# LSH attention with an MLP on one core: the hashes of batches 2 and 3 made in one stretch each, from block transposes in place, with the squares behind them

## The chip, the cores and the metric

One Trainium2 chip, one of its cores. The metric is the device time of one execution in microseconds (us), the median of several runs. The kernel before: 305.03 us (three runs, 304.65 to 305.60).

## The reference

```python
q_bits = (einsum('bhsd,dk->bhsk', q, proj) > 0)     # 6 bits for each token and head
k_bits = (einsum('bhsd,dk->bhsk', k, proj) > 0)
mask = q_bucket[:, :, :, None] == k_bucket[:, :, None, :]
scores = where(mask, q @ k.T / sqrt(D), -1e9)
attn = exp(scores - max) / (sum + 1e-9)
x = (attn @ v).transpose(0, 2, 1, 3).reshape(B, S, H * D)
xn = (x - mean) / sqrt(var + 1e-6) * g_ln
out = x + relu(xn @ w_ch1) @ w_ch2
```

B = 4 batches, H = 8 heads, S = 768 tokens, D = 64, so x is (4, 768, 512); the hidden width is 2048. A query sees only the keys whose 6 hash bits equal its own. All inputs and the output are f32.

## The kernel before, in words

**Chunks and steps.** The work goes in 12 chunks, numbered 0 to 11: 4 batches of 3 chunks of 256 tokens. A chunk has 12 attention units, three for each of four pairs of heads. A unit is a scores step S (4 matmuls, L513, into a tile of the PSUM pool ps_sc, two buffers), an exponential on ACT (L519) and a values step A (8 matmuls, L534, into ps_av). After a pair's third A, DVE divides (L564 to L572) and the pair's part of x is done. The MLP of a chunk runs one chunk later: `norm` on DVE (L626 to L628) and a transposing DMA on SP's queue (L637, xnT), 8 up steps U (8 matmuls each, L653, evicted by DVE L132 and ACT L136 in turn as hbuf), and in the chunk after that 8 down steps D (4 matmuls each, L675; four make one tile o, which DVE adds to x at L680). Up and down tiles, the hash and the share take their PSUM from one pool, ps_mm, with two buffers.

**What prepares a batch.** Each batch comes in two halves of four heads. For batches 2 and 3 each preparing step is a letter with two digits, batch and half: L loads q and k (four DMAs of 384 KB on SP, L147), W loads v (L182); N casts q and k to bf16 on POOL (L270), T transposes them by a DMA into the operand tile `slots` (L294), O places the odd tokens (L194). The hash: B is four block transposes of 32x32 on DVE (L275), from the natural tiles `qnat`, `knat` to tiles `bt`; H is the matmuls of the transposed tile with the projection (L313; 16 in the program and 32 records in the trace for a half), a threshold pass and a scaling on DVE (L321, L324) and a write of the bits to DRAM (L326, bits_d); J reads them back into `slots` (four DMAs, L333). V casts the values on POOL (L419) and sums them; E is the share, one matmul (L433) whose result DVE copies to vsum (L434). Q is four squares in place over q and k, on ACT (L218), whose sums go to the tile `sq`; a reduce of sq (L721), two small DMAs on POOL (L723, L725) and a second reduce (L733) give the flag that chooses at the very end between this kernel and a general path.

**The order.** Chunks 0 to 2 follow an order written by hand. From the third on, `interleave` goes through the units: S of the next unit, then A of this one, with fillers between them, spread by their costs. The fillers of a chunk are `norm`, the four or so last D steps of the chunk before, U steps, and the preparing steps that `plan` names for that chunk: three texts, early | late | end, which are mixed evenly with the first four tail steps, the other four, and the ups. `alone` gives steps that stand right after a unit's S: twelve places, one for each unit. Each engine takes its instructions in the order of its own list. Steps of batches 2 and 3 are kept in the order of the program; a scheduler orders the rest by priority.

Of the kernel before, what the change touches and what calls it, by code (L numbers as in the profile page):

```python
# [9 lines left out]
F32 = mybir.dt.float32  # L10
BF16 = mybir.dt.bfloat16
# [17 lines left out]
def kernel(  # L29
# [11 lines left out]
    nc = tc.nc  # L41
    P = 128

    B, H, S, D = q.shape
# [3 lines left out]
    NC = S // P  # L48
# [5 lines left out]
    CT = TT * P  # L54
# [26 lines left out]
    NG, DG = P // 32, D // 32  # L81
    proj4 = consts.tile([P, DG, 32], F32)
# [23 lines left out]
    for i in range(2):  # L106
# [3 lines left out]
    work = main.enter_context(tc.tile_pool(name="work", bufs=2))  # L110
    bounce = main.enter_context(
        tc.tile_pool(name="bounce", bufs=2, space=bass.MemoryType.DRAM)
    )
    ps_mm = main.enter_context(
        tc.tile_pool(name="ps_mm", bufs=2, space=bass.MemoryType.PSUM)
    )
    attn = ExitStack()
    nat = attn.enter_context(tc.tile_pool(name="nat", bufs=4))
    ps_sc = attn.enter_context(
        tc.tile_pool(name="ps_sc", bufs=2, space=bass.MemoryType.PSUM)  # L120
    )
# [76 lines left out]
    class Prep:  # L198
# [72 lines left out]

        def blocks(self, half, a, j):

            bt = work.tile([P, 2, NC, DG, 32], F32, tag="qkT", bufs=4, name="bt")
            done = nc.vector.transpose(  # L275
                out=bt.rearrange("p h c e j -> p (h c e j)"),
                in_=self.tiles[half]["qk"[a]][:, 2 * j : 2 * j + 2].rearrange(
                    "p h c d -> p (h c d)"
                ),
            )  # L280
            if self.b > 1:
                tc.keep_in_program_order(done)
            self.bt[half, a, j] = bt

        def pair_places(self, half):

# [16 lines left out]
            dst = self.pair_places(half)  # L303
            copy_by(eng, dst[0:D, :, 1, :], dst[D:P, :, 0, :])

        def hashes(self, half):

            NT_ = NC * 32
            hp = ps_mm.tile([P, 2, NT_], F32, tag="mm", name="hash")
            for a in range(2):  # L310
                for e in range(DG):
                    for g in range(4):
                        nc.tensor.matmul(  # L313
                            hp[32 * g : 32 * (g + 1), a, :],
                            proj4[:, e, :],
                            self.bt[half, a, g // 2][:, g % 2, :, e, :],
                            start=(e == 0), stop=(e == DG - 1),
                            skip_group_check=True,
                        )
            bits = work.tile([P, 2, NT_], BF16, tag="bits", name="bits4")  # L320
            nc.vector.tensor_scalar(  # L321
                bits, hp, scalar1=0.0, scalar2=0.5, op0=AOP.is_gt, op1=AOP.subtract
            )
            nc.vector.tensor_scalar_mul(bits, bits, 2.0 * BIT)  # L324
            bd = bounce.tile([P, 2 * NT_], BF16, tag="bits", name="bits_d")
            nc.sync.dma_start(out=bd, in_=bits.rearrange("p a n -> p (a n)"))  # L326
            self.bd[half] = bd

        def bits_home(self, half):

# [39 lines left out]
        def head_rows(self, h, engs):  # L370

            W = HS // 2
            for y, eng in zip((2, 3, 0, 1), engs):
                a, part = y // 2, y % 2
                dst = self.sl[D:K1, h, a].rearrange("p (par u t) -> p par u t", par=2, u=2)
                copy_by(eng, dst[:, :, part, :], self.head_bits[h][32 * y : 32 * y + n_bits])
# [87 lines left out]
        def part(self, kind, half):  # L464

            if kind == "T":
                return [(0, lambda: self.operands(half))]
            if kind in "Oo":
                return [(0, lambda: self.odd_tokens(half, "S" if kind == "O" else "G"))]
            if kind == "H":  # L470
                return [(1300, lambda: self.hashes(half))]
            if kind == "J":
                return [(0, lambda: self.bits_home(half))]
            if kind == "N":
                return [(0, lambda a=a: self.narrow(half, a)) for a in range(2)]
            if kind in "BK":
                return [
                    (0, lambda a=a, j=j: self.blocks(half, a, j))
                    for a in range(kind == "K", 2) for j in range(2)
                ]  # L480
            if kind == "E":
                return [(110, lambda: self.share(half))]
            if kind == "L":
                return [(0, lambda: self.load(half))]
            if kind == "W":
                return [(0, lambda: self.load_v(half))]
            if kind == "V":
                return [(0, lambda: self.values(half)), (0, lambda: self.value_sums(half))]
            return [
                (0, lambda a=a, j=j: self.squares(half, a, j)) for a in range(2) for j in range(2)  # L490
            ]
# [88 lines left out]
    def mlp_steps(b, t, x):  # L580
# [84 lines left out]
        def down(i, part):  # L665
            cut = 2 if (b, t, i) == (B - 1, NT - 1, TT - 1) else 1
            per = 4 // cut
            width = d_model // cut
            cols = slice(part // per * width, (part // per + 1) * width)
            if part % per == 0:  # L670
                st["o"] = ps_mm.tile([P, width], F32, tag="mm", name="o2")
            o2 = st["o"]
            step = NH // per
            for nt in range(part % per * step, (part % per + 1) * step):
                nc.tensor.matmul(  # L675
                    o2, st["h"][:, nt, i * P : (i + 1) * P], w2_sb[:, nt, cols],
                    start=(nt == 0), stop=(nt == NH - 1),
                )
            if part % per == per - 1:
                nc.vector.scalar_tensor_tensor(  # L680
                    x[:, i, cols], o2, st["rs"][:, i : i + 1], x[:, i, cols],
                    op0=AOP.mult, op1=AOP.add,
                )
                nc.sync.dma_start(
                    out=out[b].rearrange("(p c) d -> p c d", p=P)[:, CMAP[b][t * TT + i], cols],
                    in_=x[:, i, cols],
                )

        ups = [(900, lambda n2=n2: up(n2)) for n2 in range(NH // 2)]
        downs = [  # L690
            (870, lambda i=i, part=part: down(i, part)) for i in range(TT) for part in range(4)
        ]
        return (0, norm), ups, downs, (first_stats, first_norm, first_trans)
# [127 lines left out]
    def first_two():  # L821
# [106 lines left out]
    plan = {  # L928
# [7 lines left out]
    }  # L936

    def prepare(text):
# [6 lines left out]
    alone = {  # L945
        2: "Q01 QQQQ..",
        3: "B20 Q10 Q.Q.Q.Q.BBBB",
        4: "B21 Q11 Q.Q.Q.Q.BBBB",
        5: "Q20 Q..Q..Q..Q..",
        6: "B30 Q21 BBBBQ.Q.Q.Q.",  # L950
        7: "B31 Q30 BBBBQ.Q.Q.Q.",
        8: "Q31 Q..Q..Q..Q..",
    }

    def spread(text):
# [237 lines left out]
```

## Time and profile before

| | us |
|---|---|
| median of three runs | 305.03 |
| profiled execution | 305.38 |
| its span | 303.7 |
| busy PE | 295.2 |
| busy ACT | 215.6 |
| busy DVE | 179.8 |
| busy POOL | 91.3 |

The span runs from the first to the last instruction of the profiled execution; 1.7 us of that execution's time lie around it. Rows of the trace give the start in the span, the duration, the engine (PE matmuls, PEld weight loads, DVE, ACT, POOL; SPq and POOLq are DMA issues), the line, the operation, and the tiles written and read. A bracket at the end gives the engine's idle time before the row and what ended it. A matmul group's duration overlaps the next group's start, since matmuls are pipelined, so steps on PE are taken from start to start.

The chunks that the change touches start, by their second scores step, at 95.69 (chunk 4), 119.31 (5), 143.37 (6), 167.20 (7), 191.03 (8), 213.11 (9), 235.18 (10).

### The profile page before, as it was taken

Reading aid. Unit: us, or ns where it says so; the run is one execution under the profiler, and the core shown is the slowest. Engines: PE = TensorE matmul, PEld = TensorE weight load, DVE = VectorE, ACT = ScalarE, POOL = GpSimd, SP = SyncE. Lnnn points to the kernel's source line nnn. Section 1 sums busy time; section 2 is a strip of 40 time slices with the busy share of each in tenths; the row PEclk is TensorE's granted clock in tenths of the full one; section 3 lists DMA queues with packets and bytes.
Section 4 is the critical chain, followed back from the end, with each engine's and each line's share of the span. In section 5 each row is a group of like instructions: output and inputs, shape, how many; then the busy total and the mean of one; then the engine's idle time right before and its main releaser. Section 6 shows DMA issues by size and latency. Waiting matters only on the chain.

```text
span 303.7 us, 7929 instructions
## 1 busy us (share of the span) xinstructions
PE 295.2 (97%) x3285; PEld 224.7 (74%) x3309; DVE 179.8 (59%) x409; ACT 215.6 (71%) x273; POOL 91.3 (30%) x117
## 2 busy tenths in 40 slices
PE   8999899999999999999999999999999999999995
PEld 5677788578688688678678678679679678687564
DVE  1998678845659459634964954633733734646322
ACT  4899986967788778669578687879677667665020
POOL 3559490685403424500831730200300200201100
PEclk9999999999999999999999999999999999999999
DMA  6999999588296379777487274330110210200302
GB/s 197 367 311 252 260 256 185 120 192 260 42 141 194 89 214 200 161 231 246 140 142 205 19 154 113 21 96 2 35 71 2 64 42 2 69 37 3 106 3 73
DMA packets 64361, 40.40 MB, mean 133 GB/s; under 512 B 44864, under 2 KB 60224, under 8 KB 64320
## 3 DMA queue, kind: packets, MB, share of 16 engines
q1 hardware_dynamic: 61024, 35.64, 47.2%
q0 software_dynamic: 3216, 4.20, 7.8%
q8 instruction: 27, 0.44, 0.6%
q14 instruction: 14, 0.11, 0.1%
q10 hardware_dynamic: 80, 0.00, 0.0%
HBM read 27.97 MB, written 6.88 MB: 115 GB/s over the span
## 4 chain that ended last, share of the span: by engine, by line
PE 93%; DVE 2%; ACT 2%; DMA 1%; issue 1%; SPq 0%; DVEq 0%; ACTq 0%
PE hp L653 28%; PE o L675 27%; PE sc L513 20%; PE av L534 11%; PE hash L313 3%; PE tpose L237 2%; ACT ex L519 1%; DMA knat<-in_k_dram 1%; PE av L549 1%; DVE slots L196 1%; PE hash L384 1%; DVE xn L600 0%; DVE bits L365 0%; PE hash L356 0%; ACT slots L192 0%
## 5 line engine op out<-in xcount | busy, mean ns | idle before, releaser
L519 ACT ACTIVATE ex<-sc,expb 128x1024 bf16<-128x1024 f32 x144 | 159.0, 1114 | 55.5 <-PE sc L513 54.0
L653 PE MATMUL hp<-xnT,w_sb 128*128 128x256 bf16 x768 | 97.7, 272 | 0.1
L675 PE MATMUL o<-w_sb,hbuf 128*128 128x512 bf16 (+1 forms) x376 | 93.1, 370 | 1.0
L513 PE MATMUL sc<-slots 70*128 70x256 bf16 x576 | 87.0, 272 | 0.8 <-ACT ex L519 0.4
L653 PEld LDWEIGHTS <-w_sb 128*128 128x128 bf16 x768 | 72.4, 97 | 9.4 <-issue 0.5
L534 PEld LDWEIGHTS <-ex 128*128 128x128 bf16 x1152 | 53.4, 97 | 15.5 <-ACT ex L519 2.3
L513 PEld LDWEIGHTS <-slots 70*128 70x128 bf16 x576 | 52.0, 97 | 15.5 <-issue 2.7
L534 PE MATMUL av<-vaug,ex 128*128 128x65 bf16 x1152 | 58.0, 193 | 0.7 <-ACT ex L519 0.7
L132 DVE TENSOR_SCALAR hbuf<-hp 128x512 bf16<-128x512 f32 x47 | 32.4, 690 | 43.2 <-PE hp L653 42.5
L675 PEld LDWEIGHTS <-hbuf 128*128 128x128 bf16 x400 | 36.9, 97 | 26.6
L136 ACT ACTIVATE hbuf<-hp 128x512 bf16<-128x512 f32 x49 | 29.1, 595 | 17.8 <-PE hp L653 17.3
L680 DVE SCALAR_TENSOR_TENSOR x<-o,rs,x 128x512 f32<-128x512 f32 (+1 forms) x25 | 18.1, 725 | 31.9 <-PE o L675 31.7
L642 POOL TENSOR_SCALAR rs<-mv 128x2 f32<-128x2 f32 x11 | 7.1, 643 | 90.3 <-DVE mv L627 90.3
L419 POOL CAST vaug<-vnat 128x1536 bf16<-128x1536 f32 x6 | 8.8, 1465 | 45.6 <-DMA vnat<-in_v_dram 28.2
L564 DVE TENSOR_SCALAR rc<-av 128x4 f32<-128x4 f32 x36 | 5.7, 157 | 27.9 <-PE av L534 27.9
L572 DVE TENSOR_TENSOR x<-x,rc 128x256 f32<-128x256 f32 x36 | 17.6, 489 | 1.0
L628 DVE SCALAR_TENSOR_TENSOR xn<-x,mv,gbc 128x512 bf16<-128x512 f32 x22 | 17.7, 840 | 0.1
L565 DVE TENSOR_TENSOR x<-av,vsum 128x256 f32<-128x256 f32 x36 | 14.9, 415 | 0.0
L626 DVE BATCH_NORM_STATS2 stats<-x 128x6 f32<-128x512 f32 x22 | 14.1, 677 | 0.2
L218 ACT ACTIVATE qnat<-qnat 128x768 f32<-128x768 f32 x16 | 13.4, 839 | 0.0
L218 ACT ACTIVATE knat<-knat 128x768 f32<-128x768 f32 x16 | 13.4, 836 | 0.0
L428 POOL TENSOR_TENSOR vsum<-vsum,vaug 128x256 f32<-128x256 f32 x18 | 12.7, 708 | 1.1
(87 smaller groups left out, 208.8 us busy)
## 6 DMA issues: line engine op xcount, KB each, us to landing
out_dram<-x SPq DMA_DIRECT2D x23, 256.0 KB
vnat<-in_v_dram SPq DMA_DIRECT2D x7, 768.0 KB
qnat<-in_q_dram SPq DMA_DIRECT2D x11, 384.0 KB
knat<-in_k_dram SPq DMA_DIRECT2D x11, 384.0 KB
w_sb<-in_moe_w_ch_dram POOLq DMA_DIRECT2D x3, 1024.0 KB, 19.1
qnat<-in_q_dram SPq DMA_DIRECT2D x2, 768.0 KB
knat<-in_k_dram SPq DMA_DIRECT2D x2, 768.0 KB
slots<-slots SPq DMA_DIRECT2D x4, 384.0 KB
```

Source lines behind the costliest of these rows:

```text
L132: nc.vector.tensor_scalar_max(dst, src, 0.0)
L136: nc.scalar.activation(dst, src, AF.Relu if relu else AF.Copy)
L218: done = nc.scalar.activation(src, src, AF.Square, accum_out=sq[:, a, col : col + 1])
L513: nc.tensor.matmul(sc[:, i, :], sl[0:K1, h, 1, kj * P : (kj + 1) * P], sl[0:K1, h, 0, q0 : q0 + CT],)
L519: nc.scalar.activation(ex, sc, AF.Exp, bias=expb[:, 1:2] if b else expb[:, 0:1], scale=scale if b else scale / Q_SCALE,)
L534: nc.tensor.matmul(av[:, h - ha, qi, :], state[g][:, i, qi * P : (qi + 1) * P], va[:, h, CMAP[b][kj], :], start=((g, i, qi) == (0, 0, 0)), ...
L565: nc.vector.tensor_tensor(xv, num, vs[:, ha : ha + 2, :].unsqueeze(2).to_broadcast([P, 2, TT, D]), op=AOP.add,)
L572: nc.vector.tensor_tensor(xv, num, rc.unsqueeze(3).to_broadcast([P, 2, TT, D]), op=AOP.mult)
L628: nc.vector.scalar_tensor_tensor(xn[:, :, i, :], x[:, i, :].rearrange("p (o d) -> p o d", d=P), mv[:, i, 0:1], gbc.rearrange("p (o d) -> p ...
L653: nc.tensor.matmul(hp[:, i, :], w1_sb[:, dt, nt * P : (nt + 1) * P], st["xnT"][:, dt, :], start=(dt == 0), stop=(dt == ND - 1),)
L675: nc.tensor.matmul(o2, st["h"][:, nt, i * P : (i + 1) * P], w2_sb[:, nt, cols], start=(nt == 0), stop=(nt == NH - 1),)
L680: nc.vector.scalar_tensor_tensor(x[:, i, cols], o2, st["rs"][:, i : i + 1], x[:, i, cols], op0=AOP.mult, op1=AOP.add,)
```

## The change

For batches 2 and 3 the block transposes write over the loaded q and k. `hashes` takes one or two halves: with two, all matmuls stand in one stretch into a tile of ps_sc (not ps_mm), the threshold and the scaling are one pass each of 128x768, and the bits leave in one DMA. In the plan H20 (chunk 4) and H21 (chunk 5) become G20 in chunk 5, H30 (6) and H31 (7) become G30 in chunk 8; J20 and J21, J30 and J31 follow them. E20, E21, E30 and E31 keep their chunks. Since the squares overwrite q and k, and the hash now reads the transposed values from there, the squares of batches 2 and 3 move behind it: Q20 from chunk 5 to 6, Q21 from 6 to 7, Q30 from 7 to 8, Q31 from 8 to 9. B21 moves from the last four units of chunk 4 to the first four of chunk 5, B30 and B31 from the first to the last four units of chunks 6 and 7.

```diff
         def blocks(self, half, a, j):
-            bt = work.tile([P, 2, NC, DG, 32], F32, tag="qkT", bufs=4, name="bt")
+            nat_ = self.tiles[half]["qk"[a]][:, 2 * j : 2 * j + 2]
+            if self.b > 1:
+                bt = nat_
+            else:
+                bt = work.tile([P, 2, NC, D], F32, tag="qkT", bufs=4, name="bt")
             done = nc.vector.transpose(
...
-        def hashes(self, half):
+        def hashes(self, *halves):
             NT_ = NC * 32
-            hp = ps_mm.tile([P, 2, NT_], F32, tag="mm", name="hash")
...
+            n = len(halves)
+            if n == 1:
+                hp = ps_mm.tile([P, 2 * NT_], F32, tag="mm", name="hash").unsqueeze(1)
+            else:
+                hp = ps_sc.tile([P, n, 2 * CT], F32, tag="sc", name="hash")[:, :, 0 : 2 * NT_]
+            for i, half in enumerate(halves):
+                for a in range(2):
+                    for e in range(DG):
+                        for g in range(4):
+                            nc.tensor.matmul(
+                                hp[32 * g : 32 * (g + 1), i, a * NT_ : (a + 1) * NT_],
...
-            bits = work.tile([P, 2, NT_], BF16, tag="bits", name="bits4")
+            bits = work.tile([P, n, 2 * NT_], BF16, tag="bits", name="bits4")
...
-            bd = bounce.tile([P, 2 * NT_], BF16, tag="bits", name="bits_d")
-            nc.sync.dma_start(out=bd, in_=bits.rearrange("p a n -> p (a n)"))
-            self.bd[half] = bd
+            bd = bounce.tile([n, P, 2 * NT_], BF16, tag=f"bits{n}", name="bits_d")
+            nc.sync.dma_start(out=bd.rearrange("n p x -> p n x"), in_=bits)
+            for i, half in enumerate(halves):
+                self.bd[half] = bd[i]
...
+            if kind == "G":
+                return [(2600, lambda: self.hashes(0, 1))]
...
     plan = {
...
-        4: "H20 V20 | L21 J20 W21 | N21 T21 O21",
-        5: "H21 E20 | V21 L30 J21 | E21 W30 L31",
-        6: "V30 N30 | T30 O30 W31 | H30 E30",
-        7: "J30 V31 N31 | T31 O31 | H31 E31",
-        8: "J31",
+        4: "V20 | L21 W21 | N21 T21 O21",
+        5: "E20 | V21 L30 G20 J20 J21 | E21 W30 L31",
+        6: "V30 N30 | T30 O30 W31 | E30",
+        7: "V31 N31 | T31 O31 | E31",
+        8: "G30 J30 J31",
     }
...
     alone = {
...
-        4: "B21 Q11 Q.Q.Q.Q.BBBB",
-        5: "Q20 Q..Q..Q..Q..",
-        6: "B30 Q21 BBBBQ.Q.Q.Q.",
-        7: "B31 Q30 BBBBQ.Q.Q.Q.",
-        8: "Q31 Q..Q..Q..Q..",
+        4: "Q11 Q..Q..Q..Q..",
+        5: "B21 BBBB........",
+        6: "Q20 B30 Q.Q.Q.Q.BBBB",
+        7: "Q21 B31 Q.Q.Q.Q.BBBB",
+        8: "Q30 ....Q.Q.Q.Q.",
+        9: "Q31 Q..Q..Q..Q..",
     }
```

The lists of the engines, at three places. In the changed kernel the lines below L275 stand 4 to 11 further down (L564 is L574, L626 is L636, L434 is L442).

DVE at the start of chunk 5, before: the division of chunk 4's last pair (rc, x), the norm of chunk 4, the bits of H21, and the copy of share E20 behind the next pair's division.

```order
L570 RECIPROCAL rc<-rc 128x4
L572 TENSOR_TENSOR x<-x,rc 128x2x2x64
L626 BN_STATS stats<-x 128x6 x2
L627 BN_AGGR mv<-stats 128x2 x2
L628 SCALAR_TENSOR_TENSOR xn<-x,mv,gbc 128x4x128 x2
L321 TENSOR_SCALAR bits_2216<-hash 128x384
L324 TENSOR_SCALAR bits_2216<-bits_2216 128x384
L564 TENSOR_SCALAR rc<-av 128x4
L565 TENSOR_TENSOR x<-av,vsum_93 128x2x2x64
L570 RECIPROCAL rc<-rc 128x4
L434 COPY vsum_92<-share 128x256
```

The same place in the changed kernel.

```order
L580 RECIPROCAL rc<-rc 128x4
L582 TENSOR_TENSOR x<-x,rc 128x2x2x64
L279 STREAM_TRANSPOSE qnat<-qnat 128x768
L636 BN_STATS stats<-x 128x6 x2
L637 BN_AGGR mv<-stats 128x2 x2
L638 SCALAR_TENSOR_TENSOR xn<-x,mv,gbc 128x4x128 x2
L279 STREAM_TRANSPOSE qnat<-qnat 128x768
L442 COPY vsum_92<-share 128x256
L690 SCALAR_TENSOR_TENSOR x<-o_2147,rs,x 128x512
L279 STREAM_TRANSPOSE knat<-knat 128x768
```

Two transposes of B21 stand around the norm, the hash's bits are gone from here, and the copy of the share comes right behind the second transpose. On PE the down step after the next scores and values steps takes the PSUM buffer that this copy empties; PE's steps from the start of chunk 5 are now S D A D S E D A D S A D S D A, then the stretch of G20, then S A, half a D, S A, half a D. Before they were S D A H S A D S D A E S D A D S.

DVE at the share E30 in the ups of chunk 6, before: two bits passes of H30, then evictions of ups (hbuf), the division and the copy.

```order
L321 TENSOR_SCALAR bits_2792<-hash 128x384
L324 TENSOR_SCALAR bits_2792<-bits_2792 128x384
L132 TENSOR_SCALAR hbuf<-hp 128x512
L564 TENSOR_SCALAR rc<-av 128x4
L565 TENSOR_TENSOR x<-av,vsum_92 128x2x2x64
L570 RECIPROCAL rc<-rc 128x4
L434 COPY vsum_93<-share 128x256
```

The same place in the changed kernel.

```order
L580 RECIPROCAL rc<-rc 128x4
L132 TENSOR_SCALAR hbuf<-hp 128x512
L582 TENSOR_TENSOR x<-x,rc 128x2x2x64
L132 TENSOR_SCALAR hbuf<-hp 128x512
L279 STREAM_TRANSPOSE qnat<-qnat 128x768
L442 COPY vsum_93<-share 128x256
```

The copy now stands behind the second up's eviction and the first transpose of B30. On PE the share stands as U A S E U A U; E31 in chunk 7 stands the same way. Before, PE had the share of both chunks between steps of attention, A S E A S.

ACT at the end of chunk 8 in the changed kernel: exponentials (ex), evictions of ups (hbuf), and the squares of Q30.

```order
L218 ACTIVATE knat,sq<-knat 128x768
L529 ACTIVATE ex<-sc,expb 128x1024 x2
L218 ACTIVATE knat,sq<-knat 128x768
L136 ACTIVATE hbuf<-hp 128x512
L529 ACTIVATE ex<-sc,expb 128x1024 x2
L136 ACTIVATE hbuf<-hp 128x512
```

The same place before, where the squares are those of Q31.

```order
L136 ACTIVATE hbuf<-hp 128x512
L519 ACTIVATE ex<-sc,expb 128x1024
L218 ACTIVATE knat,sq<-knat 128x768
L136 ACTIVATE hbuf<-hp 128x512
L519 ACTIVATE ex<-sc,expb 128x1024 x2
L136 ACTIVATE hbuf<-hp 128x512
```

The last square moved from the tenth unit of the chunk to the eleventh, and there it stands ahead of the eviction that empties the PSUM buffer of the chunk's last up.

More of the change, by code (lines that the diff above doesn't have):

```diff
@@ L272, in blocks @@
         def blocks(self, half, a, j):
-            bt = work.tile([P, 2, NC, DG, 32], F32, tag="qkT", bufs=4, name="bt")
+            nat_ = self.tiles[half]["qk"[a]][:, 2 * j : 2 * j + 2]
[3 more added lines that the diff above has]
+                bt = work.tile([P, 2, NC, D], F32, tag="qkT", bufs=4, name="bt")
             done = nc.vector.transpose(
[L276 to L279, printed above, removed]
+                out=bt.rearrange("p h c d -> p (h c d)"),
+                in_=nat_.rearrange("p h c d -> p (h c d)"),
             )
@@ L282, in blocks @@
                 tc.keep_in_program_order(done)
-            self.bt[half, a, j] = bt
+            self.bt[half, a, j] = bt.rearrange("p h c (e j) -> p h c e j", j=32)
         def pair_places(self, half):
@@ L304, in odd_tokens @@
             copy_by(eng, dst[0:D, :, 1, :], dst[D:P, :, 0, :])
-        def hashes(self, half):
+        def hashes(self, *halves):
             NT_ = NC * 32
-            hp = ps_mm.tile([P, 2, NT_], F32, tag="mm", name="hash")
[L310 to L319, printed above, removed]
-            bits = work.tile([P, 2, NT_], BF16, tag="bits", name="bits4")
+            n = len(halves)
[9 more added lines that the diff above has]
+                                hp[32 * g : 32 * (g + 1), i, a * NT_ : (a + 1) * NT_],
+                                proj4[:, e, :],
+                                self.bt[half, a, g // 2][:, g % 2, :, e, :],
+                                start=(e == 0), stop=(e == DG - 1),
+                                skip_group_check=True,
+                            )
+            bits = work.tile([P, n, 2 * NT_], BF16, tag="bits", name="bits4")
             nc.vector.tensor_scalar(
```

## The prediction

> **What bounds the kernel now.** I read the page's busy times first, then its chain of what ended last, then the busy times chunk by chunk, then the single rows around the places that the change touches.
>
> ```profile
> PE 295.2 (97%) x3285; PEld 224.7 (74%) x3309; DVE 179.8 (59%) x409; ACT 215.6 (71%) x273; POOL 91.3 (30%) x117
> PE 93%; DVE 2%; ACT 2%; DMA 1%; issue 1%; SPq 0%; DVEq 0%; ACTq 0%
> 95.69:119.31 23.62, 23.46 (x276) 17.92 (x275) 15.19 (x34) 18.14 (x25) 7.79 (x9) 1.00 0.58 151
> 119.31:143.37 24.06, 23.84 (x278) 18.11 (x277) 12.67 (x33) 18.41 (x25) 5.91 (x8) 1.00 0.80 198
> 143.37:167.20 23.83, 23.73 (x277) 18.01 (x276) 16.66 (x35) 17.75 (x25) 11.05 (x12) 1.00 0.68 170
> 167.20:191.03 23.83, 23.72 (x277) 18.00 (x276) 15.95 (x35) 18.28 (x25) 7.85 (x9) 1.00 0.48 91
> 191.03:213.11 22.08, 21.97 (x244) 16.94 (x243) 10.68 (x28) 18.28 (x25) 1.71 (x2) 1.00 0.25 41
> ```
>
> The first two lines are busy times and the shares of the chain; the other five are chunks 4 to 8, each cut where its second scores step starts, with length, busy time of PE, PEld, DVE, ACT, POOL, granted clock, DMA share and GB/s. PE is busy 97% of the span, carries 93% of the chain, and inside these chunks it is idle for 0.1 to 0.2 us at most, at clock 1.00. So the time is the sum of PE's steps plus whatever makes PE wait, and everything else in the change matters only where PE waits for it. Chunk 8, with no hash and no share, lasts 22.08 us; that is the base.
>
> ```profile
> 119.75 1.03 PE L675 MATMUL o<-w_sb,hbuf 128*128 128x512 bf16 x3
> 120.61 0.41 PE L534 MATMUL av<-vaug,ex 128*128 128x65 bf16 x8
> 120.95 1.51 PE L313 MATMUL hash<-bt,proj 128*32 128x192 f32 x32
> 122.39 0.61 PE L513 MATMUL sc<-slots 70*128 70x256 bf16 x4
> ...
> 132.40 1.04 PE L653 MATMUL hp<-xnT,w_sb 128*128 128x256 bf16 x8
> 133.27 0.41 PE L534 MATMUL av<-vaug,ex 128*128 128x65 bf16 x8
> 133.52 0.60 PE L513 MATMUL sc<-slots 70*128 70x256 bf16 x4
> 133.96 0.28 PE L433 MATMUL share<-vs,epsk 128*128 128x256 bf16 x1
> 134.29 1.03 PE L653 MATMUL hp<-xnT,w_sb 128*128 128x256 bf16 x8
> ```
>
> From start to start (the second column is the pipelined duration, which overlaps the next row): down D 0.86, values A 0.25, scores S 0.44, up U 0.87. Chunk 4 has one hash H and nothing else over the base: 23.62 - 22.08 = 1.54 us for a hash, of which 1.44 from 120.95 to the next scores. Chunk 5 has a hash and two shares E: 24.06 - 22.08 - 1.54 = 0.44. From E at 133.96 to U at 134.29 is 0.33, so E is 0.11 and a wait of 0.22 stands behind the second one: 2 x 0.11 + 0.22 = 0.44. Chunks 6 and 7 have one hash and one share each: 1.54 + 0.11, and 0.10 is left as waiting.
>
> **The change, part by part.**
>
> (1) The hash in one stretch.
>
> ```profile
> L313 PE MATMUL hash<-bt,proj x192: 326/326/350, 47.9 to 181.9; 128*32 128x192 f32 x192
> ```
>
> One record takes 0.326 us, and the 32 of 120.95 last 1.51, so the last starts 1.18 after the first. Eight sets of four column groups: 1.18 / 7 = 0.17 a set. 8 x 0.17 = 1.35, so 0.09 of the 1.44 is way out and 0.10 of the 1.54 is way in. A stretch of 64 pays both once: 2 x 1.54 - 0.19 = 2.9 us. That is -0.2 per batch, **-0.4 us** for both. The bounds are 0 and -0.4, since no work goes, only an edge. This is all that PE gains.
>
> (2) Chunk 5: the down step behind the share. The new order of DVE puts both q transposes, and the norm between them, ahead of the copy that empties the share; the fifth down step takes the share's buffer.
>
> ```profile
> 119.51 0.16 DVE L564 TENSOR_SCALAR rc<-av 128x4 f32<-128x4 f32 x1
> ...
> 120.12 0.43 DVE L572 TENSOR_TENSOR x<-x,rc 128x256 f32<-128x256 f32 x1
> 120.58 1.29 DVE L626 BATCH_NORM_STATS2 stats<-x 128x6 f32<-128x512 f32 x2
> ...
> 123.32 0.55 DVE L321 TENSOR_SCALAR bits<-hash 128x384 bf16<-128x384 f32 x1
> ...
> 126.19 0.39 DVE L434 COPY vsum<-share 128x256 f32<-128x256 f32 x1
> ...
> 149.28 0.97 DVE L275 STREAM_TRANSPOSE bt<-qnat 128x768 f32<-128x768 f32 x1
> 150.17 0.94 DVE L275 STREAM_TRANSPOSE bt<-knat 128x768 f32<-128x768 f32 x1
> ```
>
> T is the chunk's start, 119.31 above. DVE begins at T+0.20, its division of the last heads lasts to 120.58 (1.07), the norm from 120.58 to 123.32 is 2.74, a transpose is 0.89 from start to start. So the copy starts at 0.20 + 1.07 + 0.89 + 2.74 + 0.89 = T+5.79, takes 0.39, and with 0.05 for the signal frees the buffer at T+6.23. PE runs S D A D S E D A D S A to that down step: 3 x 0.44 + 4 x 0.86 + 3 x 0.25 + 0.11 = T+5.62. **+0.60 us**. In the kernel before, no transpose stood there. The bounds: 0 if a transpose in place took 0.59 or less, and +1.2 if it took 1.2; I take the row of the transpose there is. The in-place form is in no trace here.
>
> (3) Chunk 5, behind the stretch: S A and half a D, twice. The stretch holds a scores buffer until its bits pass is through. That pass is 128x768: 0.55 for 384 columns here, 0.69 for the 512 of the up's eviction (133.55, below), so an estimate by that slope of 0.97; the second S is ready 0.44 + 0.25 + 0.43 = 1.12 after the stretch, the pass ends 0.11 + 0.97 + 0.05 = 1.13 to 1.17: **+0.05**. The second A needs the exponential of the first S behind the stretch. S to exponential is 0.70 (208.45 to 209.15, below), the exponential 1.11, a signal 0.05: 1.86. PE is there at 1.12 + 0.44 = 1.56. **+0.27** (0 to 0.3). In chunk 8, G30 has more between: only the +0.05.
>
> (4) Chunks 6 and 7: E30 and E31 now stand "U A S E U A U", the pattern of 133.96, where one up waits for the eviction of the up before:
>
> ```profile
> 133.55 0.69 DVE L132 TENSOR_SCALAR hbuf<-hp 128x512 bf16<-128x512 f32 x1 [0.55 <-PE hp L653]
> ```
>
> 133.55 + 0.69 + 0.05 = 134.29, the start of the waiting U: 0.22. The next U takes the share's buffer, and its copy now stands behind a transpose on DVE: on this clock 134.24 + 0.89 + 0.39 + 0.05 = 135.57, against 134.29 + 0.87 + 0.25 = 135.41, where PE is ready: 0.16. So 0.22 + 0.16 - 0.10 (what they lost before) = 0.28 each, **+0.6** for both. Bounds 0 and 1.2, the last if a whole transpose more stood uncovered in one of them.
>
> (5) Chunk 8: the squares of Q30 now fall on units 4, 6, 8, 10.
>
> ```profile
> 208.45 0.60 PE L513 MATMUL sc<-slots 70*128 70x256 bf16 x4
> 209.15 1.11 ACT L519 ACTIVATE ex<-sc,expb 128x1024 bf16<-128x1024 f32 x1 [0.62 <-PE sc L513]
> 210.16 0.83 ACT L218 ACTIVATE knat<-knat 128x768 f32<-128x768 f32 x1
> ...
> 210.98 0.59 ACT L136 ACTIVATE hbuf<-hp 128x512 bf16<-128x512 f32 x1
> ```
>
> Exponential, square, eviction in this order: 0.70 + 1.01 + 0.82 + 0.59 + 0.05 = 3.17 after the S. The last U of the chunk takes the buffer that this eviction empties and is ready after S U A U S: 2 x 0.44 + 2 x 0.87 + 0.25 = 2.87. **+0.3** (0 to 0.8, a whole square). Other squares stand before evictions with room.
>
> (6) The test of the squares. The last square moves from chunk 8 to the tenth unit of chunk 9, so the reduce m<-sq moves from 1.2 to about 20 us behind that chunk's start, and the two DMAs and the second reduce follow.
>
> ```profile
> 214.27 0.18 DVE L721 TENSOR_REDUCE m<-sq 128x2 f32<-128x32 f32 x1
> 218.63 0.58 POOL L725 DMA_DIRECT2D mr<-m_d  x1 [0.84 <-DMA m_d<-m]
> mr<-m_d POOLq DMA_DIRECT2D x1, 1.0 KB, 3.6
> 236.34 0.40 DVE L733 TENSOR_REDUCE m<-mr 1x2 f32<-1x256 f32 x1
> 239.53 1.24 SPq L637 DMA_TRANSPOSE xnT<-xn  x1
> 246.18 1.04 PE L653 MATMUL hp<-xnT,w_sb 128*128 128x256 bf16 x8
> ```
>
> 218.63 + 3.6 - 214.27 = 8 us from m to mr, so mr lands some 6 us into chunk 10. The second reduce stands inside that chunk's norm on DVE and would start 2.5 us into it: the norm, and the transposing DMA behind it, come 3.5 us later. That DMA was issued 6.65 us before its first U; 3.15 are left. **+0.1** (0 to 0.6: a landing between 2.7 and 3.7).
>
> What stays hidden: the in-place tile saves no time; the transposes of chunks 4 to 7 are the same eight (6.7 on DVE, which is 59% busy); squares move within ACT, 71%.
>
> ```profile
> 126.58 1.08 SPq L326 DMA_DIRECT2D bits_d<-bits  x1
> 131.40 5.97 SPq L333 DMA_DIRECT2D slots<-bits_d  x4
> ```
>
> On SP the write of the bits and the reads J20 come later, in chunk 5, behind the four loads L30. From the write's issue to the last of four reads went 126.58 to 137.37, 10.8 us. The write is issued about T+13.1 now (stretch ends T+11.5, bits 1.5), the first scores of batch 2 are due about T+25.4: 12.3 us. The first heads need only the first two of the four reads, so there is room of 2 to 4 us. J21, J30 and J31 have a chunk or more.
>
> **The sum.** -0.4 + 0.60 + 0.05 + 0.27 + 0.6 + 0.05 + 0.3 + 0.1 = +1.6. On the profiled execution, 305.38 us (its span is 303.7), that is 307.0; it lies 0.35 above the median of the runs shown, 305.03. So **306.6** for the median.
>
> **Rivals.**
>
> (a) Transposes quicker in place. Place: DVE ahead of the share's copies in chunks 5, 6 and 7. It decides at 0.59 us a transpose against 0.89: below that the copy of chunk 5 comes in time (0.60 goes) and the two of chunks 6 and 7 too (2 x 0.16). 306.6 - 0.92 = 305.7, no change that can be measured. For it: reads and writes share one tile. Against: all 0.94 to 0.97 rows are the same shape and type.
>
> (b) Every new wait is covered and only the saving of the stretch is left: 305.03 - 0.4 = 304.6. For it: PE's rows show waits of only 0.22 now. Against: the sums of (2) and (5) miss by 0.3 to 0.6, and the order on DVE and ACT is fixed.
>
> (c) The bits come home late: SP sends them behind 1.5 MB of L30, and the first scores of batch 2 wait. It decides where the room of 2 to 4 us is used up; DMA share is 0.80 in chunk 5, the highest. Each us late is a us of PE; I price it +1.5: 308.1.
>
> (d) POOL holds up DVE in the long DVE chain of chunk 5.
>
> ```profile
> 118.64 1.47 POOL L419 CAST vaug<-vnat 128x1536 bf16<-128x1536 f32 x1 [3.65 <-DMA vnat<-in_v_dram]
> 144.03 1.47 POOL L419 CAST vaug<-vnat 128x1536 bf16<-128x1536 f32 x1 [17.34 <-PE sc L513]
> 144.18 1.59 DVE L572 TENSOR_TENSOR x<-x,rc 128x256 f32<-128x256 f32 x1
> ```
>
> Beside the cast at 144.03 the division takes 1.59 in place of 0.43: 1.16 longer, and all of that would be added to the 0.60 of (2): 307.8. In chunk 5 the cast ended at 120.11, just as the division began at 120.12. Its values are loaded earlier now (J20 no longer goes before them on SP), so it should end earlier: against. The Trainium skill, SBUF — State Buffer, section "SBUF: two separate sides", says that VectorE and GpSimd share a port pair which one instruction holds to its end, for a VectorE operation with two SBUF inputs among others; by that rule, and the row at 144.18 agrees with it, a cast that came 1.3 us later than before would give this rival's time.
>
> **How the numbers follow.** Forecast 0.52; (a) 0.12; (b) 0.15; (c) 0.13; (d) 0.08. About 0.3% of the time, 0.9 us, is what a measurement can tell from no change: faster is under 304.1, slower over 305.95. The bounds of the forecast's terms put it between 305.7 and 307.7 in most cases; I give a tenth of it, (a) whole, and two thirds of (b) to no change: 0.05 + 0.12 + 0.10 = 0.27. A third of (b) is faster: 0.05. The rest, 0.68, is slower. The range 304.8 to 308.4 takes in (a), the forecast and (d), and half or more of (c); it leaves out most of (b) and the late end of (c), about 0.2.
>
> **What would show it.** In the changed profile: a hash row of 64 records lasting near 2.85; chunk 4 at 22.08; in chunk 5 a PE wait of 0.6 before a down row, released by DVE's copy vsum<-share, and one of 0.3 before a values row, released by ACT; in chunks 6 and 7 two waits of about 0.2 around the share; in chunk 8 one of 0.3 before its last up; the second reduce some 6 us into chunk 10. I am wrong if PE shows none of the waits (then (a) or (b)), if scores of chunk 6 wait for a DMA (then (c)), or if a DVE row in chunk 5 is stretched beside a cast (then (d)).

## The result, and the profile after

The changed kernel takes 305.79 us (median of 18 runs), the kernel before 304.90 (18 runs beside it): a ratio of 1.0033, 95% interval 1.0021 to 1.0045. So it is slower by 0.9 us; the forecast was 1.6. The profiled execution took 306.9 us with a span of 305.3.

The chain of what ended last, and chunks 4 to 8 of the changed kernel (the columns are those of the rows of before):

```profile
PE 89%; DVE 4%; ACT 3%; issue 1%; DMA 1%; SPq 0%; ACTq 0%; DVEq 0%
...
96.28:118.35 22.07, 22.07 (x246) 16.91 (x243) 11.03 (x29) 17.80 (x25) 10.72 (x12) 1.00 0.65 180
118.35:144.50 26.15, 25.65 (x312) 19.20 (x309) 16.17 (x36) 15.42 (x17) 2.32 (x3) 1.00 0.54 147
144.50:166.92 22.42, 22.42 (x248) 17.10 (x244) 16.46 (x33) 18.18 (x25) 10.38 (x11) 1.00 0.79 198
166.92:189.34 22.42, 22.42 (x248) 17.09 (x245) 16.05 (x33) 18.18 (x25) 8.32 (x10) 1.00 0.47 89
189.34:214.58 25.24, 25.10 (x310) 18.94 (x307) 12.31 (x30) 18.80 (x26) 1.72 (x2) 1.00 0.20 47
```

PE still carries the chain, but DVE and ACT have 7% of it where they had 4%: the chain leaves PE at more places. By chunks the difference to before is -1.55, +2.09, -1.41, -1.41, +3.16; chunks 9 and 10 are 22.07 and 22.08 in both. That is **+0.88 us**; the medians differ by 0.89. PE's busy time counts modelled ends, so a short wait between two matmuls shows as idle only in part: chunk 6 reads 22.42 of 22.42 busy, and two waits are in it all the same. They are found from start to start.

The stretch in chunk 5, and the two steps behind it (PE):

```profile
126.59 0.41 PE L544 MATMUL av<-vaug,ex 128*128 128x65 bf16 x8
126.93 0.86 PE L320 MATMUL hash<-qnat,proj 128*32 128x192 f32 x16
...
128.25 0.83 PE L320 MATMUL hash<-qnat,proj 128*32 128x192 f32 x16
...
129.67 0.61 PE L523 MATMUL sc<-slots 70*128 70x256 bf16 x4
...
130.36 0.59 PE L685 MATMUL o<-w_sb,hbuf 128*128 128x512 bf16 x2
130.81 0.60 PE L523 MATMUL sc<-slots 70*128 70x256 bf16 x4
131.54 0.41 PE L544 MATMUL av<-vaug,ex 128*128 128x65 bf16 x8
```

The values step of 126.59 ends its 0.25 at 126.84, the scores come at 129.67: 2.83 us for a stretch, against 2 x 1.54. The half down of 130.36 takes 0.45 in place of 0.43 (the scores buffer: 0.02), and from the scores at 130.81 to the values at 131.54 it is 0.73 in place of 0.44: 0.29 of waiting for the exponential.

The wait for the share's buffer in chunk 5 (PE, then DVE):

```profile
123.72 0.41 PE L544 MATMUL av<-vaug,ex 128*128 128x65 bf16 x8
124.43 1.02 PE L685 MATMUL o<-w_sb,hbuf 128*128 128x512 bf16 x4 [0.30 <-DVE vsum L442]
```

```profile
118.55 0.16 DVE L574 TENSOR_SCALAR rc<-av 128x4 f32<-128x4 f32 x1 [1.10 <-PE av L544]
...
119.51 0.97 DVE L279 STREAM_TRANSPOSE qnat<-qnat 128x768 f32<-128x768 f32 x1
120.40 1.24 DVE L636 BATCH_NORM_STATS2 stats<-x 128x6 f32<-128x512 f32 x2
...
123.09 0.97 DVE L279 STREAM_TRANSPOSE qnat<-qnat 128x768 f32<-128x768 f32 x1
123.99 0.39 DVE L442 COPY vsum<-share 128x256 f32<-128x256 f32 x1
```

The down step could start at 123.97 and starts at 124.43, 0.05 behind the end of the copy: 0.46. The bracket says 0.30, since it counts from the modelled end of the values step. The transposes in place take 0.97, as those into another tile did.

The shares in the ups of chunk 6 (PE, then DVE; chunk 7 is the same to 0.02):

```profile
159.93 0.28 PE L441 MATMUL share<-vs,epsk 128*128 128x256 bf16 x1
160.19 1.03 PE L663 MATMUL hp<-xnT,w_sb 128*128 128x256 bf16 x8
161.06 0.40 PE L544 MATMUL av<-vaug,ex 128*128 128x65 bf16 x8
161.38 1.03 PE L663 MATMUL hp<-xnT,w_sb 128*128 128x256 bf16 x8
```

```profile
159.45 0.69 DVE L132 TENSOR_SCALAR hbuf<-hp 128x512 bf16<-128x512 f32 x1 [1.78 <-PE hp L663]
160.06 0.97 DVE L279 STREAM_TRANSPOSE qnat<-qnat 128x768 f32<-128x768 f32 x1
160.95 0.38 DVE L442 COPY vsum<-share 128x256 f32<-128x256 f32 x1
```

The first up comes 0.15 late, 0.05 behind the eviction's end at 160.14; the second 0.07 late, 0.05 behind the copy's end at 161.33.

The end of chunk 8 (PE, then ACT):

```profile
212.72 0.60 PE L523 MATMUL sc<-slots 70*128 70x256 bf16 x4
213.47 1.03 PE L663 MATMUL hp<-xnT,w_sb 128*128 128x256 bf16 x8
```

```profile
212.01 0.83 ACT L218 ACTIVATE knat<-knat 128x768 f32<-128x768 f32 x1
...
212.83 0.59 ACT L136 ACTIVATE hbuf<-hp 128x512 bf16<-128x512 f32 x1
```

The eviction behind the square ends at 213.42, the last up starts at 213.47 in place of 213.16: 0.31.

The test of the squares (DVE, then the row of the second small DMA, whose last figure is the time from issue to landing):

```profile
241.42 0.41 DVE L743 TENSOR_REDUCE m<-mr 1x2 f32<-1x256 f32 x1 [2.12 <-DMA mr<-m_d]
```

```profile
mr<-m_d POOLq DMA_DIRECT2D x1, 1.0 KB, 2.3
```

The second reduce waited 2.1 us in the middle of the norm, and the transposing DMA was issued at 243.44, 4.2 us before its first up (247.65), 2.4 us less than before. The up starts where the values step ahead of it ends: nothing was lost.

### The profile page after: what moved, and what is told of

It reads as the page before. It is cut to its first block, busy times and chain, and to the rows that moved or that the text cites. A ratio compares the mean times of both kernels' runs of the same rounds, so it can differ in the third digit from the quotient of the medians.

```text
span 305.3 us, 7948 instructions
## 1 busy us (share of the span) xinstructions
PE 297.5 (97%) x3309; PEld 225.2 (74%) x3309; DVE 179.9 (59%) x405; ACT 215.2 (70%) x273; POOL 90.8 (30%) x117
## 4 chain that ended last, share of the span: by engine, by line
PE 89%; DVE 4%; ACT 3%; issue 1%; DMA 1%; SPq 0%; ACTq 0%; DVEq 0%
PE hp L663 27%; PE o L685 26%; PE sc L523 19%; PE av L544 11%; PE hash L320 3%; ACT ex L529 2%; PE tpose L237 2%; DMA knat<-in_k_dram 1%; PE hash L364 1%; PE av L559 1%; PE hash L392 1%; DVE xn L610 0%; DVE xn L638 0%; DVE hbuf L132 0%; DVE qnat L279 0%
## 5 line engine op out<-in xcount | busy, mean ns | idle before, releaser
L685 PE MATMUL o<-w_sb,hbuf 128*128 128x512 bf16 (+1 forms) x400 | 96.3, 370 | 0.3 <-DVE vsum L442 0.3
L652 POOL TENSOR_SCALAR rs<-mv 128x2 f32<-128x2 f32 x11 | 6.4, 579 | 97.0 <-DVE mv L637 93.8
L582 DVE TENSOR_TENSOR x<-x,rc 128x256 f32<-128x256 f32 x36 | 19.0, 527 | 1.0
L574 DVE TENSOR_SCALAR rc<-av 128x4 f32<-128x4 f32 x36 | 5.6, 155 | 20.5 <-PE av L544 20.5
L636 DVE BATCH_NORM_STATS2 stats<-x 128x6 f32<-128x512 f32 x22 | 14.2, 682 | 0.3
```

Source lines behind the costliest of these rows:

```text
L582: nc.vector.tensor_tensor(xv, num, rc.unsqueeze(3).to_broadcast([P, 2, TT, D]), op=AOP.mult)
L685: nc.tensor.matmul(o2, st["h"][:, nt, i * P : (i + 1) * P], w2_sb[:, nt, cols], start=(nt == 0), stop=(nt == NH - 1),)
```

## Experiments

Theory: the two stretches gain about 0.5 us; four kinds of waits, which the new order makes on DVE and ACT, cost about 1.4; nothing else of the change is felt. Rival: the loss lies in the stretch itself, its tile or the later bits, and the waits only stand where PE would have waited anyway. Chunk lengths tell these apart to about 0.02 us, unless a cast on POOL meets a division on DVE (last section), which added up to 0.32. The times cannot: the runs of one kernel spread over 1 us and more.

**1. One more transpose ahead of the copy.**

```diff
             nc.tensor.matmul(ps, epsk, self.vs16.rearrange("p h d -> p (h d)"))
+            if (self.b, half) == (2, 0):
+                idle = work.tile([P, 2, NC, D], F32, tag="qkT", bufs=4, name="idle")
+                done = nc.vector.transpose(
+                    out=idle.rearrange("p h c d -> p (h c d)"),
+                    in_=self.tiles[0]["q"][:, 0:2].rearrange("p h c d -> p (h c d)"),
+                )
+                tc.keep_in_program_order(done)
```

> The changed kernel with one more transpose on VectorE (of a q tile into a spare tile that nothing reads) right ahead of the copy that empties share E20 in chunk 5. Theory (the copy's place on VectorE sets the wait of the fifth down step): the wait of 0.46 us grows by one transpose, 0.89, to 1.35, and chunk 5 from 26.15 to 27.0 us; against the kernel before, +0.9 becomes +1.8 us, a ratio of 1.006. Rival (VectorE is busy 59% and has room; the 0.46 has another cause): chunk 5 stays at 26.1 to 26.2, ratio 1.003.

306.6 us, ratio 1.0053 (1.0034 to 1.0072). Chunk 5, the row of its transpose, and the down step:

```profile
118.13:145.14 27.01, 25.66 (x312) 19.20 (x309) 17.03 (x37) 15.43 (x17) 2.32 (x3) 1.00 0.53 145
...
123.77 0.94 DVE L444 STREAM_TRANSPOSE idle<-qnat 128x768 f32<-128x768 f32 x1
...
125.06 0.81 PE L692 MATMUL o<-w_sb,hbuf 128*128 128x512 bf16 x3 [1.16 <-DVE vsum L449]
```

27.01: the transpose's 0.86 from start to start came out in the chunk's length whole, and the wait is released by the same copy. DVE was busy 17.03 of 27.01 us in that chunk. How much room an engine has on average says nothing here; the order of its list does.

**2. E20 in the downs of chunk 4.**

```diff
-        4: "V20 | L21 W21 | N21 T21 O21",
-        5: "E20 | V21 L30 G20 J20 J21 | E21 W30 L31",
+        4: "V20 | L21 W21 E20 | N21 T21 O21",
+        5: "| V21 L30 G20 J20 J21 | E21 W30 L31",
```

> The changed kernel with share E20 moved from the start of chunk 5 into the downs of chunk 4, where no transpose stands on VectorE. Theory: the 0.46 us wait of the fifth down step goes, and 0.11 for the share itself moves a chunk: chunk 5 26.15 to 25.58, chunk 4 22.07 to 22.18, ratio to the kernel before 1.0015 in place of 1.003. Rival (the wait belongs to the transposes and the stretch in chunk 5 and another step takes it over, say the hash waiting for its last transposes): chunk 5 stays above 25.9.

305.67 us, ratio 1.0010 (0.9987 to 1.0034). Chunk 5; chunk 4 is 22.19:

```profile
117.88:143.46 25.58, 25.38 (x311) 19.03 (x308) 15.84 (x35) 15.44 (x17) 2.36 (x3) 1.00 0.55 147
```

To the hundredth as expected: the wait went, and no later step took it over.

**3. The squares of Q30 elsewhere.**

```diff
-        8: "Q30 ....Q.Q.Q.Q.",
+        8: "Q30 ..Q..Q.Q.Q..",
```

> The changed kernel with the squares Q30 on units 2, 5, 7 and 9 of chunk 8 in place of 4, 6, 8 and 10. Theory (the square of unit 10 stands ahead of the eviction for which the last up waits): the wait of 0.31 us goes, chunk 8 25.24 to 24.93, ratio 1.002. Rival (any four squares among the ups of a chunk with a hash make some up wait): chunk 8 stays at 25.1 to 25.3 with the wait at an earlier up.

305.62 us, ratio 1.0025 (1.0014 to 1.0036). Chunk 8:

```profile
187.81:212.81 25.00, 25.00 (x310) 19.02 (x307) 12.33 (x30) 18.13 (x25) 1.72 (x2) 1.00 0.21 47
```

0.24 of the 0.31 went. An up behind the square of unit 7 started 0.06 late instead: the rival holds for that remainder.

**4. E30 and E31 out of the ups.**

```diff
-        6: "V30 N30 | T30 O30 W31 | E30",
-        7: "V31 N31 | T31 O31 | E31",
-        8: "G30 J30 J31",
+        6: "V30 N30 | T30 O30 W31 |",
+        7: "N31 E30 V31 | T31 O31 |",
+        8: "G30 J30 J31 | E31 |",
```

> The changed kernel with shares E30 and E31 moved out of the ups: E30 into the downs of chunk 7, E31 into those of chunk 8. Theory (in U A S E U A U the first up waits for an eviction and the second for the copy behind a transpose, 0.23 in all a chunk): chunk 6 22.42 to 22.08, chunk 7 22.42 to 22.19, chunk 8 25.24 to 25.35, together -0.46 us, ratio 1.0015. Rival (a share takes one of two PSUM buffers wherever it stands, so it makes the next step wait there as well): the three chunks together lose less than 0.15 us.

305.43 us, ratio 1.0012 (0.9995 to 1.0030). Chunks 6 and 7:

```profile
144.12:166.19 22.07, 22.07 (x246) 16.91 (x243) 16.52 (x32) 18.19 (x25) 12.15 (x12) 1.00 0.79 203
166.19:188.38 22.19, 22.19 (x248) 17.02 (x244) 14.97 (x33) 18.08 (x25) 6.44 (x8) 1.00 0.42 90
```

Chunk 8 is 25.35. All as expected: among the downs a share costs its 0.11 and no wait. The edit also lets V31 and N31 change places; chunk 7 shows nothing of that.

**5. More downs behind the stretch.**

```diff
-                return [(2600, lambda: self.hashes(0, 1))]
+                return [(1740, lambda: self.hashes(0, 1))]
```

> The changed kernel with the cost that the planner gives a stretch at 1740 in place of 2600, so that more of the downs stand between the steps behind it. Theory (the second values step behind the stretch waits for an exponential that started only after it): in chunk 5 that step now has a whole down more ahead of it, the 0.29 us wait goes, chunk 5 26.15 to 25.86; the ups of chunk 8 shift too, so the square of unit 10 no longer meets the last up: 25.24 to about 24.95. Ratio 1.001. Rival (the wait is for the scores buffer that the stretch holds, or moves to the next step): chunk 5 stays above 26.0.

305.42 us, ratio 1.0019 (1.0004 to 1.0034). Chunks 5 and 8:

```profile
116.68:142.55 25.87, 25.48 (x313) 19.28 (x310) 16.16 (x36) 15.48 (x17) 2.32 (x3) 1.00 0.49 127
...
187.38:212.35 24.97, 24.97 (x310) 19.02 (x307) 12.33 (x30) 17.85 (x25) 1.72 (x2) 1.00 0.20 47
```

0.28 of the 0.29 went. Half a down, not the whole one that I expected, now stands between the second scores step and its values step (scores at 129.14, values at 130.01), and it sufficed; the half down ahead of those scores stayed. So the wait was for the exponential, not for the scores buffer. In chunk 8, 0.27 of the 0.31 went with the shift of the ups.

**6. All four waits away.** The plan of runs 2 and 4, the cost of run 5, E21 ahead of G20, and Q30 on units 2, 4, 6 and 9.

```diff
-        5: "E20 | V21 L30 G20 J20 J21 | E21 W30 L31",
+        5: "| V21 L30 E21 G20 J20 J21 | W30 L31",
...
-        8: "Q30 ....Q.Q.Q.Q.",
+        8: "Q30 ..Q.Q.Q..Q..",
```

> The changed kernel with all four waits taken away: E20 in the downs of chunk 4, E21 in those of chunk 5, E30 in chunk 7, E31 in chunk 8, Q30 on units 2, 4, 6 and 9, the stretch's cost 1740. Theory (nothing but these waits made the change slower): chunks 4 to 8 are 22.18, 25.03, 22.08, 22.19, 25.03, together 116.5 against 117.4 of the kernel before and 118.3 of the changed one: ratio 0.997, about 304.0 us. Rival (the gain of the stretch is lost elsewhere, in the tail or in late bits): the ratio stays at or over 0.9995.

304.40 us, ratio 0.9978 (0.9962 to 0.9994). Chunks 4 to 8:

```profile
96.34:118.52 22.18, 22.18 (x247) 17.01 (x244) 11.46 (x30) 17.81 (x25) 10.49 (x12) 1.00 0.65 179
118.52:143.55 25.03, 25.03 (x312) 19.07 (x308) 15.56 (x35) 15.39 (x17) 2.42 (x4) 1.00 0.53 140
143.55:165.62 22.07, 22.07 (x246) 16.92 (x243) 15.77 (x32) 18.19 (x25) 12.11 (x12) 1.00 0.80 217
165.62:187.81 22.19, 22.19 (x247) 17.03 (x244) 14.97 (x33) 18.08 (x25) 6.44 (x8) 1.00 0.42 90
187.81:212.84 25.03, 25.03 (x312) 19.07 (x309) 12.74 (x31) 18.20 (x25) 1.71 (x2) 1.00 0.21 47
```

116.50, as expected, 1.80 less than the changed kernel and 0.92 less than the kernel before. The stretch itself is sound; what surrounded it cost more than it gained. But not all of the 0.92 is the stretch's, since this plan also takes away waits that the kernel before had; run 7 sorts them.

**7. The kernel before, with E20 and E21 in the downs.** Four single hashes stay.

```diff
-        4: "H20 V20 | L21 J20 W21 | N21 T21 O21",
-        5: "H21 E20 | V21 L30 J21 | E21 W30 L31",
+        4: "H20 V20 | L21 J20 W21 E20 | N21 T21 O21",
+        5: "H21 | V21 L30 E21 J21 | W30 L31",
```

> The kernel before, with four single hashes, and only shares E20 and E21 moved into the downs of chunks 4 and 5, as in the run with all four waits taken away. It tells what that run owes to the shares and what to the stretch. Theory: chunk 5 loses the 0.22 us wait behind its second share and the 0.11 of the first, which goes to chunk 4: chunks 4 to 8 are 23.73, 23.73, 23.83, 23.83, 22.08, together 117.2: ratio 0.9993, and 0.7 us over the run with the stretches. Rival (shares in the downs are what makes the other run fast, not the stretch): 116.5 to 116.7 here as well.

304.35 us, ratio 0.9992 (0.9975 to 1.0009). Chunk 4; chunk 5 is 23.73:

```profile
94.70:118.64 23.94, 23.89 (x279) 18.08 (x276) 15.70 (x35) 18.14 (x25) 7.50 (x8) 1.00 0.64 151
```

Chunk 5 is as expected; chunk 4 is 0.21 longer. Late in it a cast on POOL met a division on DVE, and an up waited for the eviction behind that division:

```profile
112.95 1.48 POOL L270 CAST nat<-knat 128x1536 bf16<-128x1536 f32 x1
...
113.61 1.09 DVE L572 TENSOR_TENSOR x<-x,rc 128x256 f32<-128x256 f32 x1
...
116.22 1.03 PE L653 MATMUL hp<-xnT,w_sb 128*128 128x256 bf16 x8
```

The division took 1.09 us in place of 0.42, the eviction behind it ended at 116.17, and the up started 0.05 later, 0.22 behind the end of its values step (115.76 + 0.24). In the profile of the kernel before, the same division took 0.78, at no cost to PE. Such a meeting hangs on when a load lands (last section). With chunks 6 to 8 (23.84, 23.83, 22.08) the sum is 117.42, that of the kernel before; less the 0.21 it is the 117.2 that I expected. So the two shares alone are worth about 0.2, and the rival (116.5 to 116.7) falls. The 0.92 of run 6 then adds up: 0.50 from the two stretches (2 x (3.08 - 2.83)), 0.22 from the wait behind E21, and 0.20 from the waits of 0.10 behind E30 and E31, all three of which the kernel before had as well. The times of runs 6 and 7 do not tell the two apart; their intervals overlap.

**8. Run 6 with the first values of batch 2 loaded earlier.**

```diff
-        2: "| H11 E10 W11 o10 V11 L20 | J10 N11 T11 o11 N20",
-        3: "J11 E11 T20 W20 O20 | |",
+        2: "| H11 E10 W11 o10 V11 L20 | J10 N11 T11 o11 N20 W20",
+        3: "J11 E11 T20 O20 | |",
```

> The run with all four waits taken away, and the load of batch 2's first values (W20) issued at the end of chunk 2 in place of chunk 3. Theory (a division on VectorE and a cast on GpSimd that meet hold each other up; in chunk 3 the cast begins when the load lands, at 90.2 to 91.3 us in four of the seven profiles with transposes in place, over the division at about 91, so chunk 3 takes 22.18 to 22.50): the cast comes some 10 us earlier, clear of that division, which takes 0.42, and chunk 3 is 22.18; chunks 4 to 8 stay at 116.5. Ratio to the kernel before 0.997. Rival (the division is long for another reason, or the cast meets the next division): a division over 0.9 us and chunk 3 over 22.25.

303.92 us, ratio 0.9964 (0.9952 to 0.9977): 1.0 us under the kernel before and the lowest median here. Half a miss: the cast left the division at about 91 us, but at 79.14 it met another, which took 1.60. That one cost PE nothing: chunk 3 is 22.19, and chunks 4 to 8 are 116.49. Whether run 8 is faster than run 6 is not shown: the intervals overlap.

**9. G20 as two hashes.**

```diff
-                return [(2600, lambda: self.hashes(0, 1))]
+                return [(2600, lambda: self.hashes(0, 1))] if self.b > 2 else [(1300, lambda: self.hashes(0)), (1300, lambda: self.hashes(1))]
```

> The changed kernel with G20 as two hashes of one half each, through the pool of the ups and downs, one after the other; G30 stays a stretch. Theory (a stretch saves only one way in and one way out): the two take 1.54 each, 3.08 against 2.84 in one stretch; behind them the waits for the exponential (0.29) and the scores buffer (0.02) go, since each hash stands with steps of its own between; chunk 5 is 26.15 + 0.24 - 0.31 = 26.1. Rival (the sets of a stretch run faster, or the change of pool matters): the two take under 2.95 or over 3.2.

305.84 us, one run. Chunk 5, and the first hash from its way in to the scores behind it:

```profile
117.40:143.46 26.06, 25.48 (x308) 19.08 (x309) 16.27 (x38) 15.29 (x17) 2.33 (x3) 1.00 0.53 140
...
125.64 0.41 PE L544 MATMUL av<-vaug,ex 128*128 128x65 bf16 x8
125.97 0.86 PE L320 MATMUL hash<-qnat,proj 128*32 128x192 f32 x16
...
127.41 0.61 PE L523 MATMUL sc<-slots 70*128 70x256 bf16 x4
```

127.41 - 125.64 - 0.25 = 1.52, and the second hash takes 1.54 in the same way: 3.06 against 2.83 in one stretch, within what the theory expected. The stretch saves its edges and nothing more, and no effect of the pool shows. (Chunk 4 is 22.34 in this profile, in place of 22.07, by another meeting of a cast and a division.)

## Why the prediction was right, and where its sizes were off

The direction and each place were right but the last, and no cost came out more than 0.02 over its forecast.

| term | forecast | measured | from |
|---|---|---|---|
| (1) two stretches | -0.4 | -0.50 | 2 x (2.83 - 3.08) |
| (2) down step behind E20 | +0.60 | +0.46 | 124.43 - 123.97; runs 1 and 2 |
| (3) scores and values behind G20 | +0.05, +0.27 | +0.02, +0.29 | rows; run 5 |
| (3) scores behind G30 | +0.05 | +0.02 | chunk 8: 25.24 = 22.08 + 2.83 + 0.31 + 0.02 |
| (4) shares in the ups, chunks 6 and 7 | +0.6 | +0.26 | 2 x (0.23 - 0.10); run 4 |
| (5) last up of chunk 8 | +0.3 | +0.31 | 213.47 - 213.16; run 3 |
| (6) test of the squares | +0.1 | 0 | chunk 10: 22.08 |
| sum | +1.6 | +0.86 | chunks: +0.88 |

**What was too large.** About half of the 0.7 is in (4). I put the transpose behind the full 0.69 of the eviction; from start to start that eviction is 0.61 (159.45 to 160.06), and it began 1.08 us behind the start of its up, where the row that I took (133.55) stands 1.15 behind its own. So the first wait came out at 0.15 for 0.22 and the second at 0.07 for 0.16, in both chunks. In (2) the chain ahead of the first transpose was 0.96 (118.55 to 119.51), not 1.07: 1.07 was the start of the norm, which waits for the division's end as the transpose does not. The norm was 2.69, not 2.74. That wait is the difference of two chains of about 6 us; a few hundredths in each link make a fourth of it.

In (6) I took 3.6 us for the landing of the second small DMA, from its old place. At the new place it landed in 2.3, and in 2.0 to 2.4 in all nine profiles with the new plan, against 3.6 and 3.3 in the two with the old one; why is not shown. So the second reduce waited 2.1, not 3.5. That the transposing DMA lands in 2.7 to 3.7, as the range of (6) has it, no view shows; the runs show only that 4.2 us before its first up were enough.

In (1) the gain went past the bound that I gave it, 0.25 a stretch for 0.19: a set of four column groups takes 0.165 us (eight sets from 126.93 to 128.25), not 0.17, which leaves more to the edges. And chunks 4 to 7 have twelve transposes, not the eight that I counted as hidden; they are twelve in both kernels, so the sum does not change.

**The rivals.** (a) falls: a transpose in place takes 0.97. By the time alone it would have stood, since its 305.7 is nearer to the measured 305.79 than the forecast's 306.6; only the rows, with the waits at their places, decide between the two. (b) falls for the changed kernel, but its premise, that the stretch alone would be a gain, is what run 6 shows. (c) did not come: chunk 6 starts without a wait for a DMA; run 6 carries the same reads of the bits and has none either. (d) did not come in chunk 5. Casts did stretch divisions elsewhere: in chunk 3 at a cost to PE (last section), in chunks 6 and 7 (to 1.30, 1.31 and 1.09) at none.

**A trap in the comparison.** The spans differ by 1.6 us, just what I forecast, yet only 0.88 of it is the change. Chunk 4 started 0.59 later in this execution (96.28 against 95.69): 0.27 of it was there when chunk 3 started (73.78 against 73.51), and 0.32 came in chunk 3. In eleven profiles of eleven kernels chunk 4 starts anywhere from 94.60 to 96.34, and both ends belong to kernels with the new plan. Two single profiles would have confirmed a sum that was nearly twice the true one.

## What to carry to other kernels

When a short instruction that frees a buffer moves behind long ones on an in-order engine, the work that waits for that buffer is late by their length less the room that it had, however idle the engine is on average: read the order of the list, not the busy share. Joining two steps of the bound engine gained only their edges here (0.25 us a pair), while each step moved around them can open a wait; so after such a change look from start to start for waits of 0.1 to 0.5 us, and move the waiting steps one by one. Compare stretches of the trace rather than whole spans. And before 0.2 or 0.3 us in a stretch is put down to the change, look whether two other engines met by chance there.

## What the runs showed of the hardware that I had not expected

A division on DVE and a cast on POOL that meet hold each other up, whichever comes second. In chunk 3 of the changed kernel's profile (POOL, DVE, PE):

```profile
91.22 1.46 POOL L427 CAST vaug<-vnat 128x1536 bf16<-128x1536 f32 x1 [11.17 <-DMA vnat<-in_v_dram]
...
91.23 1.72 DVE L582 TENSOR_TENSOR x<-x,rc 128x256 f32<-128x256 f32 x1
...
93.61 1.03 PE L663 MATMUL hp<-xnT,w_sb 128*128 128x256 bf16 x8 [0.16 <-DVE hbuf L132]
```

The division began 0.01 behind the cast and ended 0.27 behind its end; the eviction behind it was late, and an up with it: chunk 3 took 22.50 in place of 22.18. In chunk 3 of run 7 the division came first:

```profile
89.99 1.74 POOL L419 CAST vaug<-vnat 128x1536 bf16<-128x1536 f32 x1 [11.22 <-DMA vnat<-in_v_dram]
...
89.98 0.42 DVE L572 TENSOR_TENSOR x<-x,rc 128x256 f32<-128x256 f32 x1
```

There the division took its usual 0.42 and the cast 1.74 in place of 1.47. The cast begins when its load lands, and that differs from execution to execution, so the meeting is a matter of chance. It made chunk 3 longer in three of these profiles (22.24, 22.37, 22.50 in place of 22.18), and chunk 4 in those of run 7 (0.21) and run 9 (0.27, a division of 1.68). The Trainium skill, SBUF — State Buffer, section "SBUF: two separate sides", has it that the port pair shared by VectorE and GpSimd goes to whichever starts first for its whole instruction, for a VectorE operation with two SBUF inputs, as this division has, among others. The two pairs of rows above agree with that in their order. In size they fall short of it: the late division ended 0.27 us behind the cast though it takes 0.42 alone, and the late cast lost 0.27, not the division's 0.42. The forecast had put the whole stretching, 1.16 us, on PE in its rival (d). In the rows above the division lost 1.30 and PE 0.32, because the eviction behind the division had about 1.0 us of room.
